# Fused attention and token/channel mixing: the last half of batch 0's attention is added up on VectorE, with another order of loads and conversions around chunk 0

## The chip, the cores and the metric

The kernel runs on one core of a Trainium2 chip. The metric is the device time of one execution in microseconds. The kernel before has a median of 2022.69 us over 3 runs (2022.31 to 2022.91).

## What is computed

The reference, cut to what matters (B=8 batches, S=4096 tokens, D=192 features, H=8 heads, K=7 taps, all fp32):

```python
w = softmax(weight_gen)                      # over the 7 taps, per token and head
x_att[b, s, h, :] = sum_k w[b, s, h, k] * x_pad[b, s + k, h, :]
h = relu(x_att.T @ w_tok1) @ w_tok2          # token mixing: 4096 -> 256 -> 4096
u = x_att + h.T
out = u + relu(u @ w_ch1) @ w_ch2            # channel mixing: 192 -> 1536 -> 192
```

## The kernel before, in words

**Tiles and stages.** A batch is cut into 8 chunks of 512 tokens (`NCH = 8`), so there are 64 chunks, numbered m over all batches. For a chunk, `token1(m)` adds the chunk's share of `x_att.T @ w_tok1` to the sum `th`/`h1s` of its batch; when the eighth chunk of a batch has been added, `make_h1` applies the relu and splits the result into a high and a low fp32r part (`h`). Only then can `token2` of that batch begin: it seeds a PSUM tile `up` with the attention output (`seed_up`), adds `h1 @ w_tok2` to it, and the sum is `u`. The channel mixing of a chunk, in the units (g, p), is products `ph` from `u` and `w_ch1`, a relu and split into `h` by ScalarE (L774) and VectorE (L778), and products `acc` from `h` and `w_ch2`. TensorE matmuls of 64 rows run in pairs on two halves of the array (`emit`, L633).

**Conversions.** The weights arrive raw and are converted in the kernel. A weight block costs three passes on ScalarE (L192, L194, L195) and a shift on VectorE (L191); weights that are split also take a cast to the high part (GpSimd L215 or ScalarE L210) and a subtraction on VectorE (L211; L595 and L596 for `w2s`). `act(what, n)` and `dve(what)` issue the next n passes of a block on that engine, `rest(what)` the rest of its job. The blocks are `("tok", m)` (w_tok1), `("w1", n)` and `("c2", n)` (w_ch1 and w_ch2), `("w2", n)` (w_tok2).

**The prologue, batch 0.** Before any channel mixing, the attention of batch 0 is done in 16 half chunks, i = 0 to 15, in an order written out by hand (tables `loads`, `fetches`, `ahead`, `behind`, `after`, L1144 to L1155). For half i: `product(i)` on VectorE multiplies taps 0 to 4 (L424, 1920 elements a partition), `product_aside(i)` on GpSimd multiplies taps 5 and 6 and adds them (L424, L435), both into the buffer `prk`, of which there are two. `sums(i)` adds the taps on TensorE by transposing matmuls into PSUM (L441, `tapsum`), ScalarE copies the sum (L463), TensorE turns it back (`turn_back`, L441) and ScalarE copies it to `xa` (`keep_turned`, L478). `token1_half(i)` (L1122) multiplies `xa` with the token weights into `th`. The sum is also stored for the residual (`store_sum`, a GpSimd DMA). For the last half, i = 15, VectorE first folds taps 3 to 5 onto 0 to 2 (`fold`, L446), so that TensorE needs 9 matmuls instead of 18. After `token1_half(15)` and four spare matmuls (L1223) comes `make_h1(0)` (ScalarE L609, VectorE L611), `first_token2` (TensorE `acc<-w,h`, L710), `first_u` (ScalarE L726 to L734, VectorE L727 to L733), and then the first `ph` products of chunk 0.

**The steady part.** From there a planner sets the order: it keeps an estimated time for each engine (`at[...]`), and `pump` (L952) places side work (conversions, attention of later batches, output moves L860) from chains by cost and due time. A token1 of a later batch is taken up when its inputs are ready by the planner's estimate (`token1_ready`), in two blocks of 64-row pairs wrapped around channel-mixing units (`emit`, L633). `begin_token2(m)` (L1312) makes sure that the batch's h1 exists: as long as it does not, it issues the missing token1 in one piece, with 128-row matmuls (`whole_token1`, L1305, matmuls on L1303), directly ahead of token2. `TURN` (L672) says behind how many thirds of the `acc` products the first `up` of a chunk is put in chunk 0.

```python
def begin_token2(m):
    need(lambda: m in w2t and m in xbt, ("w2", m))
    while m // NCH not in h1t:
        need(token1_ready, ("w1", state["token1"] + 1), ("x", state["token1"] + 1))
        whole_token1(begin_token1())

def end_token1(tok):
    ...
    pump(end + SLACK_M, (), end + SLACK_A)
    next(tok["it"], None)
```

Of the kernel before, what the change touches and what calls it, by code (L numbers as in the profile page):

```python
# [12 lines left out]
F32 = mybir.dt.float32  # L13
# [10 lines left out]
def mixer_kernel(ctx: ExitStack, tc: tile.TileContext, x, wg, wt1, wt2, wc1, wc2, out):  # L24
    nc = tc.nc
# [390 lines left out]
    def tap_product(i, wn, k0, k1, multiply):  # L416
# [7 lines left out]
        multiply(prt[i][:, k0:k1].rearrange("p k t (h g) -> p k (t h) g", h=H), x_k, w.broadcast_to([P, k1 - k0, HT * H, G]))  # L424
# [18 lines left out]
    def fold(i):  # L443

        pr = prt[i]
        nc.vector.tensor_add(pr[:, 0:FOLD], pr[:, 0:FOLD], pr[:, FOLD:2 * FOLD])  # L446

    def sums(i):
# [4 lines left out]
        for k in range(KD + 1 if i < 2 * NCH - 1 else FOLD):  # L453
            for j in range(NB):
                transpose(ps[:, j * P:(j + 1) * P], flat[:, k, j * P:(j + 1) * P], k + j == 0)
# [17 lines left out]
    def keep_turned(i):  # L473

        m, h = divmod(i, 2)
        if h == 0:
            new_xa(m)
# [194 lines left out]
    TURN = 2  # L672
# [47 lines left out]
    def first_u(up, between):  # L720
# [11 lines left out]
        dve.tensor_copy(hi[e, 1], uc[c])  # L732
        dve.tensor_sub(lo[c, 1], uc[c], hi[c, 1].bitcast(F32))  # L733
# [336 lines left out]
    with tc.tile_pool(name="pro", bufs=1) as pro, \  # L1070
# [42 lines left out]
        def rest(what):  # L1113
            for item in job(what):
                item[2]()

        def token1_half(i):
            m, h = divmod(i, 2)
            w = vals[m][0].rearrange("p (c r) -> p c r", c=CT)
            for r in range(KR):  # L1120
                for c in range(HT * h, HT * h + HT):
                    nc.tensor.matmul(th[:, r, 0:D], w[:, c, r * P:(r + 1) * P], xat[m][:, c, :],  # L1122
                                     start=m + c == 0, stop=m == NCH - 1 and c == CT - 1, skip_group_check=True)
# [5 lines left out]
        def fetch(what):  # L1129
# [48 lines left out]
        for i in range(2 * NCH):  # L1178
# [344 lines left out]
```

## Time and profile before

| | value |
|---|---|
| median of 3 runs | 2022.69 us |
| profiled execution, its own time | 2022.73 us |
| span of that execution | 2021.0 us |
| TensorE busy | 2005.3 us, 99% of the span |
| VectorE busy | 1480.0 us, 73% |
| ScalarE busy | 1297.9 us, 64% |
| GpSimd busy | 240.7 us, 12% |
| granted clock of TensorE, mean | 0.999 |

The profile is of one execution. A row of the timeline is one instruction, or several alike in a row (x8), with its start, its duration, its engine, its line in the code, the tiles out<-in and, in brackets, how long the engine had been idle before it and who released it. Times in the rows count from the span's start; 1.7 us of the execution lie outside the span. A busy time of TensorE says that a matmul was in the pipeline, and an idle time in brackets is where it truly waited.

### The profile page before, as it was taken

The numbers are of one execution on the slowest core, as the hardware profiler recorded it, in microseconds if no ns is written. First come the engines' busy times: TensorE is split into PE (matmuls) and PEld (weight loads), VectorE is DVE, ScalarE is ACT, GpSimd is POOL, SyncE is SP. The second block draws the span as 40 slices with busy tenths as digits, with TensorE's granted clock in tenths as the row PEclk, the third lists the DMA queues.
The fourth block names the chain that finished last, engine by engine and source line by source line (L and its number), as shares of the span: only waits on it lengthen the run. The fifth ranks groups of instructions, "written<-read, shape, count | busy, mean of one in ns | idle before, by whom it ended". The sixth has DMA issues, their size and how long they took to land.

```text
span 2021.0 us, 42824 instructions
## 1 busy us (share of the span) xinstructions
PE 2005.3 (99%) x18123; PEld 1702.3 (84%) x18123; DVE 1480.0 (73%) x1742; ACT 1297.9 (64%) x2033; POOL 240.7 (12%) x304
## 2 busy tenths in 40 slices
PE   9999999999999999999999999999999999999999
PEld 8788899888888888888888888888888888888887
DVE  8789999998877887777887777877777774443433
ACT  7877657566566566566566566566566566566555
POOL 7511111111101110001101011101011100000000
PEclk9999999999999999999999999999999999999999
DMA  9968787887676666676766676766676763222121
GB/s 365 341 200 235 207 232 227 232 222 214 200 211 185 187 186 171 166 212 178 193 186 166 172 206 189 189 184 162 178 211 171 192 162 106 70 74 64 48 66 25
DMA packets 172798, 362.99 MB, mean 180 GB/s; under 512 B 28735, under 2 KB 113983, under 8 KB 156862
## 3 DMA queue, kind: packets, MB, share of 16 engines
q1 hardware_dynamic: 138014, 228.01, 36.7%
q0 software_dynamic: 34304, 132.00, 26.8%
q8 instruction: 143, 2.34, 0.5%
q14 instruction: 49, 0.40, 0.1%
q10 hardware_dynamic: 288, 0.23, 0.0%
HBM read 223.60 MB, written 71.30 MB: 146 GB/s over the span
## 4 chain that ended last, share of the span: by engine, by line
PE 91%; DVE 4%; DMA 2%; ACT 2%; issue 1%; POOL 0%; ACTq 0%; DVEq 0%
PE acc L633 40%; PE ph L633 36%; PE up L633 7%; PE th L633 6%; DMA space<-in_x_dram 1%; DVE prk L424 1%; DVE h L778 1%; DMA s<-vals 1%; DVE pr L282 1%; DMA raw<-in_moe_w_ch_dram 0%; PE tapsum L441 0%; PE acc L1303 0%; DVE val L191 0%; DMA w<-s 0%; PE th L1122 0%
## 5 line engine op out<-in xcount | busy, mean ns | idle before, releaser
L633 PE MATMUL acc<-h,w2s 64*128 64x512 f32 x7500 | 1631.4, 387 | 0.0
L633 PEld LDWEIGHTS acc<-h,w2s 64*128 64x128 f32 x7500 | 1308.6, 184 | 138.8
L633 PE MATMUL ph<-u,w_hi 64*128 64x512 f32 x4608 | 1354.4, 388 | 2.4 <-DVE h L778 1.9
L633 PEld LDWEIGHTS ph<-u,w_hi 64*128 64x128 f32 x4608 | 766.2, 184 | 87.5 <-DVE h L778 3.0
L633 PE MATMUL ph<-u,w_lo 64*128 64x512 f32 x2304 | 803.1, 386 | 0.3 <-DVE w_lo L211 0.3
L774 ACT ACTIVATE h<-ph 128x1024 fp32r<-128x1024 f32 x384 | 393.8, 1026 | 569.0 <-PE ph L633 561.7
L778 DVE SCALAR_TENSOR_TENSOR h<-ph,h 128x1024 fp32r<-128x1024 f32 x384 | 464.7, 1211 | 258.3 <-ACT h L774 257.2
L633 PEld LDWEIGHTS ph<-u,w_lo 64*128 64x128 f32 x2304 | 384.5, 184 | 39.2 <-DVE w_lo L211 0.7
L282 DVE TENSOR_TENSOR pr<-space,wg 128x768 f32<-128x768 f32 x336 | 313.2, 945 | 0.6 <-DMA xa<-pr 0.4
L304 POOL DMA_DIRECT2D xa<-pr x166 | 141.4, 852 | 1357.0 <-DVE pr L296 841.7
L633 PE MATMUL up<-w,h 64*128 64x512 f32 x1240 | 291.5, 386 | 0.0
L633 PEld LDWEIGHTS up<-w,h 64*128 64x128 f32 x1240 | 228.1, 184 | 23.3 <-ACT up L699 0.3
L860 ACT COPY out_tile<-oa 32x256 f32<-32x256 f32 x504 | 203.5, 404 | 6.7
L689 DVE TENSOR_TENSOR uf<-up,uf 64x512 f32<-64x512 f32 x63 | 43.0, 683 | 172.9 <-ACT uf L688 166.9
L296 DVE TENSOR_TENSOR pr<-pr 128x768 f32<-128x768 f32 x168 | 159.2, 948 | 1.9
L633 PEld LDWEIGHTS th<-xh,w 64*128 64x128 f32 x1548 | 119.4, 185 | 7.8
L633 PE MATMUL th<-xh,w 64*128 64x384 f32 (+2 forms) x1548 | 123.5, 298 | 0.0
L860 ACT COPY out_tile<-oc 32x256 f32<-32x256 f32 x252 | 101.5, 403 | 5.7 <-DVE oc L853 1.1
L850 DVE STREAM_TRANSPOSE oa<-acc 128x512 f32<-128x512 f32 x63 | 45.0, 714 | 66.2 <-PE ph L633 63.6
L699 ACT COPY up<-xb 128x1024 f32<-128x1024 f32 x56 | 56.9, 1016 | 34.7 <-DVE h L778 34.7
L841 ACT COPY acc<-uf 128x512 f32<-128x512 f32 x126 | 70.2, 591 | 0.7 <-DVE oa L850 0.3
L282 DVE TENSOR_TENSOR xa<-space,wg 128x768 f32<-128x768 f32 x56 | 53.0, 946 | 4.0 <-DMA space<-in_x_dram 3.8
(126 smaller groups left out, 1338.2 us busy)
## 6 DMA issues: line engine op xcount, KB each, us to landing
w<-s SPq DMA_DIRECT2D x96, 1024.0 KB, 6.4
xa<-pr POOLq DMA_DIRECT2D x166, 384.0 KB, 5.7
space<-in_x_dram POOLq DMA_DIRECT2D x54, 960.0 KB, 8.3
out_dram<-out_tile SPq DMA_DIRECT2D x128, 192.0 KB, 3.3
xb<-xs SPq DMA_DIRECT2D x368, 64.0 KB, 6.4
xs<-t SPq DMA_DIRECT2D x56, 384.0 KB, 3.7
raw<-in_moe_w_tok_dram SPq DMA_DIRECT2D x16, 1024.0 KB, 10.8
s<-w POOLq DMA_DIRECT2D x8, 1024.0 KB, 8.3
```

The costliest lines, as they stand in the source:

```text
L282: nc.vector.tensor_mul(t.rearrange("p t (h g) -> p (t h) g", h=H).rearrange("p (o n) g -> p o n g", o=1), x_k, w)
L296: nc.vector.tensor_add(sums[m], sums[m], prt.pop(m))
L304: nc.gpsimd.dma_start(xat[m].rearrange("p t d -> p (t d)"), sums[m].rearrange("p t d -> p (t d)"), accum_op=ALU.add)
L424: multiply(prt[i][:, k0:k1].rearrange("p k t (h g) -> p k (t h) g", h=H), x_k, w.broadcast_to([P, k1 - k0, HT * H, G]))
L633: ins = nc.tensor.matmul(out_, w, x_, start=start, stop=False, skip_group_check=True).ins
L689: nc.vector.tensor_add(u[c, 1, :], up[c, 1, :], u[c, 1, :])
L699: nc.scalar.copy(up.rearrange("p k (n b c) -> p (k n) c b", c=CT, b=Q), xb.rearrange("p k (n c b) -> p (k n) c b", c=CT, b=Q))
L774: nc.scalar.activation(h[:, :, 0, :], ph, AF.Relu)
L778: nc.vector.scalar_tensor_tensor(h[:, :, 1, :], ph, 0.0, h[:, :, 0, :].bitcast(F32), op0=ALU.max, op1=ALU.subtract)
L841: nc.scalar.copy(acc_t[g][n], u[:, n])
L850: nc.vector.transpose(ua, acc[0])
L860: nc.scalar.copy(dst, src[to:to + Q].rearrange("p (n e d) -> p n e d", n=2, d=Q)[:, n])
```

## The change

**Last half chunk.** `product(15)` no longer goes into `prk` but into the tail of another buffer, `space`. GpSimd multiplies tap 5 into that tail and tap 6 straight into `xa` (`last_aside`), without an add. VectorE adds everything up (`last_sum`): one add of 1152 elements and three of 384. The half reaches `xa` without TensorE and ScalarE. `token1_half(15)` is issued before `token1_half(14)`; three transposes of the finished half (`last_turn`) and a ScalarE copy remain for the store. The four spare matmuls go.

**Loads and conversions.** The third pass of token block 7 moves behind the copy of half 11, its shift from i=15 to i=14; the fetch of `("w2", 1)` moves from i=10 to behind `w1[2]`, `c20` and `c21`; the stores s5 and s6 move to i=14, s7 behind the relu; the loads xb1, x of batch 1 and wg8 move from i=13 and 14 to behind `first_token2`; the conversion of `w1[2]` begins ahead of `first_u`; those of `c2` and `("w2", 1)` are spread over later units. `TURN` goes from 2 to 3.

The diff, cut:

```diff
+    def last_aside(i):
+
+        m, h = divmod(i, 2)
+        new_xa(m)
+        n = 2 * FOLD * HC
+        pr = prt[i] = space[:, 2 * X1 - n:2 * X1].rearrange("p (k t d) -> p k t d", k=2 * FOLD, t=HT)
+        to = xat[m][:, HT * h:HT * h + HT, :]
+        tap_product(i, wnt, KD, KD + 1, nc.gpsimd.tensor_mul)
+        tap_product(i, wnt, KD + 1, K, nc.gpsimd.tensor_mul, to)
+
+    def last_sum(i):
+
+        m, h = divmod(i, 2)
+        pr, to = prt.pop(i), xat[m][:, HT * h:HT * h + HT, :]
+        add = nc.vector.tensor_add
+        add(pr[:, 0:FOLD], pr[:, 0:FOLD], pr[:, FOLD:2 * FOLD])
+        add(pr[:, 0], pr[:, 0], pr[:, 1])
+        add(to, to, pr[:, 2])
+        add(to, to, pr[:, 0])
...
-    TURN = 2
+    TURN = 3
...
-                 9: [w2, "xb0"], 10: [("w2", 1)], 11: [w1[2]], 12: ["c20", ("c2", 1)], 13: ["xb1", 8], 14: ["wg8"]}
-        fetches = {3: ["s0"], 5: ["s1"], 7: ["s2"], 8: ["s3"], 11: ["s4"], 13: ["s5"], 14: ["s6"], 15: ["s7"]}
+                 9: [w2, "xb0"], 11: [w1[2]], 12: ["c20", ("c2", 1)], 13: [("w2", 1)]}
+        fetches = {3: ["s0"], 5: ["s1"], 7: ["s2"], 8: ["s3"], 11: ["s4"], 14: ["s5", "s6"]}
...
-                 11: [(tok[7], 1)], 12: [(w1[1], 1)], 13: [(w2, 1)], 14: [(w2, 1)]}
+                 11: [(tok[7], 1)], 12: [(tok[7], 1), (w1[1], 1)], 13: [(w2, 1)], 14: [(w2, 1)]}
...
-        for i in range(2 * NCH):
+        for i in range(2 * NCH - 1):
...
-        store_sum(i // 2)
-        keep_turned(i)
+        i += 1
+        product(i)
+        last_sum(i)
+        dve(w2)
+        keep_turned(i - 1)
+        seed_up(0, up, xbt[0], (1,))
+        act(w2)
+        token1_half(i)
+        token1_half(i - 1)
+        last_turn(i)
+        dve(w1[0])
+        dve(w2)
+        make_h1(0, th[:, :, 0:D])
+        rest(w1[0])
+        load("s7")
         rest(w2)
-        token1_half(i)
-        spare = ps_pro.tile([P, 512], F32, tag="turn", name="turn", bufs=2)
-        for _ in range(4):
-            nc.tensor.matmul(spare[:, 0:2 * P], w1_hi[:, 0, 0:P], w1_hi[:, 0, 0:2 * P], start=True, stop=True)
-        make_h1(0, th[:, :, 0:D])
+        dve(w1[1])
+        keep_sum(i)
+        act(w1[2], 2)
...
-    first_u(up, lambda: act(w1[2]))
-    act(w1[2], 2)
-    act(c2)
-    rest(w1[1])
-    dve(w1[2])
+    load_xt(1)
+    load_x(NCH)
+    load_wg(NCH)
+
+    def between():
+        act(w1[2])
+        act(c2)
+        rest(w1[1])
+    first_u(up, between, lambda: dve(w1[2]))
+    rest(w1[2])
...
-    state["vals"], state["few"] = 2, 3
+    state["vals"], state["few"] = 1, 2
...
-    first = {0: ((w1[2], ""),), 1: ((c2, "aa"), (c2, "vw")),
-             2: ((c2, ""), (w21, "aaa"), (w21, "vw"), (c21, "aaa"), (c21, "vw"), (w21, ""), (c21, ""), (c22, "aa")),
-             3: ((c22, "a"), (c22, "vw")), 4: ((c22, ""),)}
+    first = {2: ((c2, "aa"), (c2, "vw"), (c21, "aaa"), (c2, ""), (c21, "vw"), (w21, "aa"), (c21, "")),
+             3: ((w21, "a"), (w21, "vw"), (c22, "aa")), 4: ((w21, ""), (c22, "a"), (c22, "vw")), 5: ((c22, ""),)}
```

The new lines shift the old ones: L424 becomes L425, L441 L442, L609 L633, L633 L657, L664 L688, L699 L723, L774 L799, L778 L803, L860 L885 and L1303 L1339.

**What moves.** VectorE at the end of the prologue, from the last token shift (`vals`) to the two splits of h (`h`, L611). Before:

```order
L191 SCALAR_TENSOR_TENSOR vals<-vals,few 128x1024
L424 TENSOR_TENSOR prk<-xt,acc 128x1920 x2
L446 TENSOR_TENSOR prk<-prk 128x1152
L191 SCALAR_TENSOR_TENSOR vals<-vals,few 128x1024
L191 SCALAR_TENSOR_TENSOR val<-val,few 128x1024
L191 SCALAR_TENSOR_TENSOR val<-val,few 128x768 x2
L211 TENSOR_TENSOR w_lo<-val,w_hi 128x3x256
L211 TENSOR_TENSOR w_911<-val,w_911 128x1024
L611 SCALAR_TENSOR_TENSOR h_927<-th,h_927 128x2x128
```

And now:

```order
L425 TENSOR_TENSOR prk<-xt,acc 128x1920
L191 SCALAR_TENSOR_TENSOR vals<-vals,few 128x1024
L425 TENSOR_TENSOR space<-xt,acc 128x1920
L459 TENSOR_TENSOR space<-space 128x1152
L460 TENSOR_TENSOR space<-space 128x384
L461 TENSOR_TENSOR xa<-xa,space 128x384
L462 TENSOR_TENSOR xa<-xa,space 128x384
L191 SCALAR_TENSOR_TENSOR val<-val,few 128x1024
L191 SCALAR_TENSOR_TENSOR val<-val,few 128x768
L211 TENSOR_TENSOR w_880<-val,w_880 128x1024
L635 SCALAR_TENSOR_TENSOR h_896<-th,h_896 128x2x128
```

The last product has left `prk`, the fold is followed by three adds, and one shift and one split have moved behind the splits of h.

ScalarE around the first relu and u, from the copy of half 14 (`xa`) on. Before:

```order
L478 COPY xa<-turn 128x384
L463 COPY sum<-tapsum 128x3x128
L697 COPY acc<-xb_77 128x8x64
L210 CAST w_911<-val 128x1024
L478 COPY xa<-turn 128x384
L609 ACTIVATE h_927<-th 128x2x192
L726 CAST u<-acc 128x512
L728 COPY uf<-acc 64x512
L192 ACTIVATE few<-raw 128x768
L731 CAST u<-uf 64x512
L734 CAST u<-u 64x512
L194 ACTIVATE few<-raw 128x768
```

And now:

```order
L502 COPY xa<-turn 128x384
L721 COPY acc<-xb_77 128x8x64
L210 CAST w_880<-val 128x1024
L633 ACTIVATE h_896<-th 128x2x192
L487 COPY sum<-tapsum 128x3x128
L192 ACTIVATE few<-raw 128x768
L194 ACTIVATE few<-raw 128x768
L750 CAST u<-acc 128x512
L752 COPY uf<-acc 64x512
L195 ACTIVATE val<-raw 128x768
L192 ACTIVATE few<-space 128x768
L755 CAST u<-uf 64x512
```

The copy of the last sum has moved behind the relu, the copy of the last turn is gone, and four conversion passes stand ahead of the second u cast where one stood.

The end of batch 1, just ahead of token2 of chunk 8. ScalarE before, from the copy of the last token sum (`h1s`) on:

```order
L664 COPY h1s<-th 128x2x192
L609 ACTIVATE h_3937<-h1s 128x2x192
L699 COPY up<-xb_77 128x8x4x32
L774 ACTIVATE h<-ph 128x2x512
L860 COPY out_tile<-oc 32x8x32 x2
L860 COPY out_tile<-oa 32x8x32 x4
L860 COPY out_tile<-oc 32x8x32 x2
```

And now, from the copy of the last but one token sum:

```order
L688 COPY h1s<-th 128x2x192
L668 COPY th<-h1s 128x2x192
L885 COPY out_tile<-oc 32x8x32 x2
L885 COPY out_tile<-oa 32x8x32 x4
L885 COPY out_tile<-oc 32x8x32 x2
L885 COPY out_tile<-oa 32x8x32 x4
L688 COPY h1s<-th 128x2x192
L633 ACTIVATE h_3964<-h1s 128x2x192
L723 COPY up<-xb_77 128x8x4x32
L799 ACTIVATE h<-ph 128x2x512
```

TensorE in the same place, now:

```order
L657 MATMUL acc<-h,w2s 128x512
L657 MATMUL ph<-u,w_hi 128x512
L1339 MATMUL th<-xa,val 128x192 x8
L657 MATMUL up<-w_3595,h_3964 128x512
L657 MATMUL acc<-h,w2s 128x512
L657 MATMUL up<-w_3595,h_3964 128x512
```

The last token1 of the batch (m=15) has become one whole block directly ahead of the `up` matmuls that need its relu, and twelve output moves stand ahead of the copy that starts that relu. The end of batch 2 (m=23, 16 matmuls) has the same form; in the kernel before, neither batch has it.

## Rows read from the trace of the kernel before

**Rows 1.** The page: busy time of each engine, share of the span, instructions.

```profile
PE 2005.3 (99%) x18123; PEld 1702.3 (84%) x18123; DVE 1480.0 (73%) x1742; ACT 1297.9 (64%) x2033; POOL 240.7 (12%) x304
```

**Rows 2.** Waits of TensorE, 75 us to the end: total us, times, longest.

```profile
PE ph L633 <- DVE h L778: 1.9, 3, 1.2
PE th L633 <- ACT th L644: 1.4, 1, 1.4
```

**Rows 3.** Windows: length, busy PE, PEld, DVE, ACT, POOL, clock, DMA share, GB/s.

```profile
110.00:220.00 110.00, 109.77 (x996) 91.66 (x998) 103.25 (x123) 84.36 (x127) 15.95 (x22) 1.00 0.78 214
```

**Rows 4.** Timeline of VectorE, end of the prologue: start us, us, instruction.

```profile
59.60 2.14 DVE L424 TENSOR_TENSOR prk<-xt,acc 128x1920 f32<-128x1920 f32 x1
64.11 2.15 DVE L424 TENSOR_TENSOR prk<-xt,acc 128x1920 f32<-128x1920 f32 x1 [2.37 <-POOL prk L435]
67.40 1.36 DVE L446 TENSOR_TENSOR prk<-prk 128x1152 f32<-128x1152 f32 x1 [1.14 <-POOL prk L435]
68.68 1.22 DVE L191 SCALAR_TENSOR_TENSOR vals<-vals,few 128x1024 uint32<-128x1024 uint32 x1
```

**Rows 5.** Line L668 (a VectorE add of 384): duration ns min/median/max.

```profile
L668 DVE TENSOR_TENSOR h1s<-h1s x6: 545/546/548, 555.4 to 1771.8; 128x384 f32<-128x384 f32 x6
```

**Rows 6.** Timeline of TensorE from the last token products to chunk 1.

```profile
70.06 1.52 PE L1122 MATMUL th<-xa,vals 128*128 128x192 f32 x8
71.42 0.49 PE L441 MATMUL turn<-ident,sum 128*128 128x128 f32 x3
72.64 1.57 PE L1122 MATMUL th<-xa,vals 128*128 128x192 f32 x8 [0.72 <-ACT xa L478]
74.78 2.96 PE L710 MATMUL acc<-w,h 128*128 128x512 f32 x10
77.67 0.50 PE L633 MATMUL ph<-u,w_hi 64*128 64x512 f32 x2
...
86.14 0.50 PE L633 MATMUL ph<-u,w_hi 64*128 64x512 f32 x2 [1.25 <-DVE h L778]
```

**Rows 7.** Timeline of ScalarE around the first relu and u.

```profile
72.10 0.48 ACT L478 COPY xa<-turn 128x384 f32<-128x384 f32 x1
74.24 0.49 ACT L609 ACTIVATE h<-th 128x384 fp32r<-128x384 f32 x1 [1.66 <-PE th L1122]
77.00 0.59 ACT L726 CAST u<-acc 128x512 fp32r<-128x512 f32 x1 [2.27 <-PE acc L710]
78.31 0.90 ACT L192 ACTIVATE few<-raw 128x768 uint32<-128x768 uint32 x1
...
81.18 1.07 ACT L194 ACTIVATE few<-raw 128x768 f16<-128x768 f32 x1
```

**Rows 8.** Timeline of GpSimd, products of the last half.

```profile
64.58 1.70 POOL L424 TENSOR_TENSOR prk<-xt,wg 128x384 f32<-128x384 f32 x2
66.36 1.01 POOL L435 TENSOR_TENSOR prk<-prk 128x384 f32<-128x384 f32 x1
```

**Rows 9.** Timeline of TensorE at the ends of batches 1 and 2.

```profile
305.26 1.46 PE L633 MATMUL th<-xa,val 64*128 64x192 f32 x15
306.43 0.52 PE L633 MATMUL ph<-u,w_hi 64*128 64x512 f32 x1
...
583.95 0.41 PE L633 MATMUL ph<-u,w_hi 64*128 64x512 f32 x1
...
588.29 0.39 PE L633 MATMUL up<-w,h 64*128 64x512 f32 x1
```

**Rows 10.** Timeline of ScalarE at the ends of batches 1 and 2.

```profile
308.84 0.48 ACT L664 COPY h1s<-th 128x384 f32<-128x384 f32 x1 [0.33 <-PE th L633]
...
310.27 1.02 ACT L699 COPY up<-xb 128x1024 f32<-128x1024 f32 x1 [0.40 <-DVE h L778]
...
584.15 0.80 ACT L664 COPY h1s<-th 128x768 f32<-128x768 f32 x1
```

**Rows 11.** Line L860 (output moves): duration ns min/median/max.

```profile
L860 ACT COPY out_tile<-oa x504: 401/403/409, 122.3 to 2006.6; 32x256 f32<-32x256 f32 x168
```

More of the change, by code (lines that the diff above doesn't have):

```diff
@@ L414, in mixer_kernel, with tap_product @@
     FOLD = (KD + 1) // 2
-    def tap_product(i, wn, k0, k1, multiply):
+    def tap_product(i, wn, k0, k1, multiply, to=None):
         m, h = divmod(i, 2)
@@ L423, in tap_product @@
         w = w[:, j * CT + HT * h:j * CT + HT * h + HT, :, first:first + k1 - k0].rearrange("p t (h o) k -> p k (t h) o", o=1)
-        multiply(prt[i][:, k0:k1].rearrange("p k t (h g) -> p k (t h) g", h=H), x_k, w.broadcast_to([P, k1 - k0, HT * H, G]))
+        to = prt[i][:, k0:k1] if to is None else to.rearrange("p (o t) d -> p o t d", o=1)
+        multiply(to.rearrange("p k t (h g) -> p k (t h) g", h=H), x_k, w.broadcast_to([P, k1 - k0, HT * H, G]))
     def product(i):
@@ L441, in transpose, with last_turn @@
         nc.tensor.matmul(out, data, ident, is_transpose=True, start=start, stop=True, skip_group_check=True)
-    def fold(i):
-        pr = prt[i]
-        nc.vector.tensor_add(pr[:, 0:FOLD], pr[:, 0:FOLD], pr[:, FOLD:2 * FOLD])
+    def last_aside(i):
[14 more added lines that the diff above has]
+        add(to, to, pr[:, 0])
+    def last_turn(i):
+        m, h = divmod(i, 2)
+        ps = sum_ps[i] = ps_pro.tile([P, 512], F32, tag="sum", name="tapsum", bufs=2)
+        flat = xat[m][:, HT * h:HT * h + HT, :].rearrange("p t d -> p (t d)")
+        for j in range(NB):
+            transpose(ps[:, j * P:(j + 1) * P], flat[:, j * P:(j + 1) * P], j == 0)
     def sums(i):
@@ L452, in sums @@
         flat = pr.rearrange("p k t d -> p k (t d)")
-        for k in range(KD + 1 if i < 2 * NCH - 1 else FOLD):
+        for k in range(KD + 1):
             for j in range(NB):
@@ L475, in keep_turned @@
         m, h = divmod(i, 2)
-        if h == 0:
+        if m not in xat:
             new_xa(m)
@@ L718, in new_u, with first_u @@
         return t[:, 0], t[:, 1]
-    def first_u(up, between):
+    def first_u(up, between, then):
         hi, lo = new_u(0)
@@ L732, in first_u @@
         dve.tensor_copy(hi[e, 1], uc[c])
+        then()
         dve.tensor_sub(lo[c, 1], uc[c], hi[c, 1].bitcast(F32))
@@ L1122, in token1_half @@
                     nc.tensor.matmul(th[:, r, 0:D], w[:, c, r * P:(r + 1) * P], xat[m][:, c, :],
-                                     start=m + c == 0, stop=m == NCH - 1 and c == CT - 1, skip_group_check=True)
+                                     start=m + c == 0, stop=i == 2 * NCH - 2 and c == HT - 1, skip_group_check=True)
         def store_val(m):
@@ L1188, in mixer_kernel @@
                 run(islice(soft[i // 4 + 1], 3))
-            if i == 2 * NCH - 1:
-                fold(i)
             for what in after.get(i, ()):
                 dve(what)
-            if i == 15:
-                rest(w1[0])
             sums(i)
-            if i + 1 < 2 * NCH:
-                product_aside(i + 1)
+            (product_aside if i < 2 * NCH - 2 else last_aside)(i + 1)
             if i > 0:
@@ L1234, in mixer_kernel @@
     land_c2(2, "out", out_tile)
-    first_u(up, lambda: act(w1[2]))
-    act(w1[2], 2)
-    act(c2)
-    rest(w1[1])
-    dve(w1[2])
+    load_xt(1)
[7 more added lines that the diff above has]
+    rest(w1[2])
     nc.gpsimd.memset(uf_[0][DC:P, 1, :], 0.0)
+    store_sum(NCH - 1)
     load_xt(2)
-    state["vals"], state["few"] = 2, 3
+    state["vals"], state["few"] = 1, 2
     state["jobs"] = deque((convert_w2, i) for i in range(2, NCH))
```

4 lines of the change are left out of this document (2 added, 2 removed).

## The prediction, made blind

> **What bounds the kernel now.** I read the page first: TensorE is busy 99% of the span, VectorE 73%, ScalarE 64% [rows 1]. So the time changes only where TensorE's work or its waits change. Next the waits of TensorE behind the prologue: only a few microseconds in all, 1.9 for VectorE's h in three places and one wait of 1.4 for a ScalarE copy of `th` [rows 2]. The change can gain little there; what it can gain is the pace of the prologue's end, and what it can lose is new waits. A window shows the one stretch where another engine is as full as TensorE: from 110 to 220 us VectorE works 103.25 of 110.00 us [rows 3]. The timelines then give the chain at the end of the prologue: VectorE waits 2.37 us for a `prk` buffer that GpSimd holds, and 1.14 us more before the fold [rows 4]; TensorE adds and turns, ScalarE copies `xa` until 72.58, the last token product runs, and the relu starts at 74.24 [rows 6, 7]. All sums are against the profiled execution, 2022.73 us, which is 0.04 above the median.
>
> **1. The last half on VectorE: -2.7.** The product of half 14 ends at 61.74 (59.60 + 2.14). The next product does not need `prk` now, so the wait of 2.37 goes; the shift of 1.22 that stood behind the fold comes first, to 62.96, then the product of 2.15, to 65.1 [rows 4]. GpSimd's first product (tap 5, half of 1.70) is there at about 65.4 and its second at 66.3; the add of 1.01 is gone [rows 8]. So the fold of 1.36 runs from 65.4 to 66.8 [rows 4]. The three adds of 384 elements have no row of their own; the nearest row is another VectorE add of 128x384 with 0.55 each [rows 5], so `xa` is ready at about 68.4, where the ScalarE copy had it at 72.58 [rows 7]. Who is late next is half 14: its `xa` comes by TensorE and ScalarE as before, and its product started at 70.06 [rows 6]. That is why the order of the two matters: product 15 now runs in front of it (1.36 us from start to the turn behind, 70.06 to 71.42 [rows 6]), product 14 behind, done at about 71.5. The relu then starts at about 71.55 in place of 74.24. The following `acc` started 0.54 after the relu and the first `ph` 2.89 after that [rows 6]; kept, the first `ph` is at 75.0 in place of 77.67. Ahead of the u cast ScalarE now does the copy of the last sum (about 0.48) and two passes of 0.90 and 1.07. From 71.55 they and the relu (0.49) last until 74.5; the cast started 2.76 after the relu, which would be 74.3 [rows 7]. So 0.2 at most of that is in the way.
>
> Behind that, TensorE waits 1.25 before 86.14 for VectorE's first h [rows 6]. The second u block comes later relative to `ph` (four conversion passes on ScalarE ahead of its cast where one was), the splits of weights come earlier; I expect one pause of about that size in chunk 0 again, a little earlier or later. So I take the gain of the first `ph` as it is, **-2.7**. Bounds: -4.0 if that pause of 1.25 goes as well, and -0.5 if the later `up` seed and the later u block give back nearly all.
>
> **2. Edits at nothing.** The four spare matmuls ran while TensorE waited for the relu. The fetch of `("w2", 1)` now stands on SP's queue behind the last pass of `w1[2]`; its first reader is a conversion in a later unit, and if that cover fails its price is some tenths, inside the bounds of part 1. On GpSimd's queue the stores s5 to s7 pass the last products: the second product has over a microsecond in hand before the adds need it. The loads of xb1, of batch 1's x and of wg8 leave SP's queue earlier and come back behind `first_token2`; their readers are the second `up` and batch 1's attention. `TURN` puts ten `up` matmuls behind forty `acc` instead of thirty; the number of matmuls is the same, and the seed gets more time.
>
> **3. The wait of 1.4 for `th`: -0.6.** That copy stood on ScalarE behind casts of u [rows 2]. In the new order fewer casts stand ahead of it. Bounds: 1.4 gained, or 0.5 lost where another block meets the same queue. I take a little under half, because token blocks of batch 1 still meet casts of u.
>
> **4. The end of batch 1: +2.7.** The planner now takes up the last token1 of batch 1 too late to wrap it, and issues it whole, directly ahead of the `up` that needs its relu. TensorE runs its queue in order, so it has nothing to do from the end of `th` until this chain is done: start of the copy 0.33 after `th`, copy 0.48, relu 0.49 (the same line in the prologue), seed 1.02 [rows 7, 10]. That is 2.3. Before, a whole unit lay in that gap. The twelve output moves ahead of the copy last 12 x 0.403 = 4.84 [rows 11]; they start behind two copies at about 309.8 and are done at 314.7, while the unit of over 4.3 and the whole block end later, so they cost nothing here. The block itself: two prologue products of the same size from start to start, 2 x 1.36 = 2.7 [rows 6], against two wrapped blocks of 1.17 each (305.26 to 306.43 [rows 9]), 0.36 more. Together **+2.7**; bounds +2.0 (half the seed runs ahead of the relu's end) and +3.2 (the moves are late).
>
> **5. The end of batch 2: +3.8.** The same form with wider tiles: copy 0.80 [rows 10], an add of 0.55 on VectorE [rows 5], relu about 0.5, seed 1.02, and 0.33 ahead: 3.2. Here the moves are late: from 584.15 the copy, a cast and a copy of the same width (about 0.8 each) and 4.84 of moves end at 591.4; the unit from 583.95 to 588.29 and a block of 2.7 end at 591.0 [rows 9, 10]. That makes 3.4, and the block itself 0.36 more. **+3.8**; bounds +3.0 and +4.4.
>
> **The sum.** -2.7 - 0.6 + 2.7 + 3.8 = +3.2, that is 2022.73 + 3.2 = **2025.9 us**. Within 0.2%, about 4 us (2018.7 to 2026.7), this kernel's measurement can hardly tell it from no change. The forecast's own range, from half of each bound, is 2023.5 to 2028.0.
>
> **Rivals.**
>
> *The early gain is kept in full (chance 0.18).* The pause of 1.25 in chunk 0 and the wait of 1.4 both go, and the batch ends cost 2.7 and 3.6: 2022.73 - 4.0 - 1.4 + 6.3 = 2023.6. For it: the weights' splits and the h of chunk 0 have more slack behind an earlier relu [rows 4, 6]. Against: the pause hangs on VectorE's h, whose queue holds what was moved behind `first_u`.
>
> *VectorE gives the early gain back (0.18, slower).* The conversions of c2 and `("w2", 1)` move from the first units into later ones, up to 220 us, where VectorE has only 110.00 - 103.25 = 6.75 us free [rows 3]. If the moved shifts and splits (1.22 each [rows 4]) come in front of h, TensorE waits for h there. It decides from the point where five or six of them fall into that stretch. Then -2.7 and -0.6 are gone: 2022.73 + 6.5 = 2029.2. Against: TensorE waited only 1.9 us for h in the whole run [rows 2].
>
> *The sum is not earlier (0.07, slower).* If GpSimd's products for half 15 land as late as its add did (67.4 [rows 4, 8]), or VectorE's adds cost twice the row's 0.55, `xa` is no earlier than half 14's, and the relu gains nothing: 2022.73 - 0.6 + 6.5 = 2028.6.
>
> *The clock falls behind the new pauses (0.05, slower).* The longest waits in the rows are 1.25 to 1.4 us and the granted clock is 1.00 around them [rows 2, 3, 6]; a pause of 3.4 has no row. If the clock went to 1.2 GHz after the pause of batch 2, a unit of 4.3 us [rows 9] would take as long again: 2025.9 + 4.3 = 2030.2. The Trainium skill ("TensorE: Matmul & The Clock Gate", Part 1: The HAM clock gate) says that the clock is halved after TensorE has been idle for a while. It speaks against this change, but no row here shows a halved clock behind a wait, so it gets a small chance.
>
> *The batch ends cost only half (0.06, faster).* If each pause were half as long and the early gain whole: 2022.73 - 5.4 + 3.1 = 2020.4 or less.
>
> **How the numbers follow.** The forecast has 0.46, of which about 0.06 lies above 2026.7. Slower: 0.18 + 0.07 + 0.05 + 0.06 = 0.36. Faster by over 0.2% needs over 4 us, more than all of the early bounds less one batch end: 0.06. The rest, 0.58, is within 0.2%. The range goes from 2020.4 (the last rival) to 2029.6 (VectorE's rival with a little above it); the clock's case and the faster tail are left out.
>
> **What would show it.** Right: the first `ph` near 75.0; whole `th` matmuls of batch 1 and 2 with a wait of TensorE for the `up` seed or h of 2.3 and 3.4 us behind each; no other new wait over 1 us; granted clock 1.00. Wrong: no wait at those two places, waits for h between 110 and 220 us, or a first `ph` at 77.

## The result, and the profile after

The changed kernel takes 2033.08 us (median of 6 runs, 2032.06 to 2034.6), the kernel before 2022.72 us (6 runs, 2022.31 to 2022.91). The ratio is 1.0052, 95% interval 1.0039 to 1.0065: about 10.4 us slower, outside the range of the prediction. The profiled execution took 2034.60 us with a span of 2032.8 us.

The page and the waits of TensorE behind 70 us, which answer to [rows 1, 2]:

```profile
PE 2010.5 (99%) x18078; PEld 1689.3 (83%) x18078; DVE 1485.0 (73%) x1745; ACT 1298.3 (64%) x2032; POOL 239.4 (12%) x303
```

```profile
PE up L657 <- ACT up L723: 6.3, 2, 4.0
PE ph L657 <- DVE h L803: 3.2, 3, 2.2
```

The wait of 1.4 for the copy of `th` is gone. In its place stand two waits for the seed of `up`, 6.3 us together, and one of 2.2 for h. TensorE is also busy 5.2 us longer (2010.5 against 2005.3) on 45 recorded matmuls fewer. Where the time came in is read from the first `up` matmul of each chunk in the two timelines of TensorE (the end is that of the twentieth):

| chunk | `up` before, us | `up` after, us | later by |
|---|---|---|---|
| 2 | 120.96 | 119.14 | -1.8 |
| 3 | 149.06 | 148.33 | -0.7 |
| 6 | 246.16 | 243.74 | -2.4 |
| 7 | 279.51 | 279.62 | +0.1 |
| 8, start | 312.88 | 315.61 | +2.7 |
| 8, end | 317.60 | 322.06 | +4.5 |
| 9 | 343.39 | 345.46 | +2.1 |
| 15 | 527.36 | 529.56 | +2.2 |
| 16, start | 557.77 | 566.63 | +8.9 |
| 16, end | 562.47 | 574.32 | +11.9 |
| 62 | 1943.45 | 1955.32 | +11.9 |

Behind chunk 16 nothing changes any more. From chunk 9 to 15 the change looks 2.4 us better than it is, since the wrapped token blocks of batch 2 run one chunk later there and one of them is still owed. So the ledger of this execution is: up to chunk 7, +0.1; the start of chunk 8, +2.6; its twenty `up` matmuls, which take 6.45 in place of 4.72, +1.7; then to the start of chunk 16 from +4.5 to +8.9, +4.4; its `up`, 7.69 in place of 4.70, +3.0. Together 11.8.

The two places in the timeline of TensorE, and ScalarE's chain in each:

```profile
310.45 2.87 PE L1339 MATMUL th<-xa,val 128*128 128x192 f32 x16
315.61 0.50 PE L657 MATMUL up<-w,h 64*128 64x512 f32 x1 [2.30 <-ACT up L723]
...
560.07 2.52 PE L1339 MATMUL th<-xh,w 128*128 128x384 f32 x16
566.63 0.79 PE L657 MATMUL up<-w,h 64*128 64x512 f32 x1 [4.04 <-ACT up L723]
```

```profile
311.94 1.65 ACT L885 COPY out_tile<-oa 32x256 f32<-32x256 f32 x4
313.62 0.48 ACT L688 COPY h1s<-th 128x384 f32<-128x384 f32 x1
314.12 0.52 ACT L633 ACTIVATE h<-h1s 128x384 fp32r<-128x384 f32 x1
314.56 1.01 ACT L723 COPY up<-xb 128x1024 f32<-128x1024 f32 x1
...
562.04 1.65 ACT L885 COPY out_tile<-oa 32x256 f32<-32x256 f32 x4
563.72 0.80 ACT L688 COPY h1s<-th 128x768 f32<-128x768 f32 x1
565.14 0.52 ACT L633 ACTIVATE h<-h1s 128x384 fp32r<-128x384 f32 x1 [0.62 <-DVE h1s L692]
565.57 1.01 ACT L723 COPY up<-xb 128x1024 f32<-128x1024 f32 x1
```

At the second place TensorE ends the whole block at 562.6, ScalarE's copy starts only at 563.72 because the output moves last until then, and the add, the relu and the seed follow. A window table shows what the pauses left behind (columns as in [rows 3]; the clock is the number ahead of the last two):

```profile
314.00:316.00 2.00, 0.39 (x4) 0.34 (x6) 0.63 (x2) 1.97 (x4) 0.00 (x0) 1.00 1.01 199
316.00:318.00 2.00, 2.00 (x16) 1.58 (x14) 1.46 (x2) 1.44 (x2) 0.00 (x0) 0.69 0.98 320
318.00:320.00 2.00, 2.00 (x14) 1.55 (x12) 2.00 (x3) 0.00 (x0) 0.00 (x0) 0.50 0.93 228
320.00:322.00 2.00, 2.00 (x20) 1.69 (x18) 0.63 (x1) 0.00 (x0) 0.00 (x0) 0.96 0.98 408
...
566.00:570.00 4.00, 3.37 (x16) 2.68 (x18) 2.77 (x5) 2.24 (x3) 0.00 (x0) 0.50 1.03 262
570.00:574.00 4.00, 4.00 (x26) 3.10 (x26) 1.38 (x2) 0.00 (x0) 0.85 (x1) 0.65 1.02 377
```

A granted clock of 0.50 is 1.2 GHz in place of 2.4. From 316 to 322 and from 570 to 574 TensorE is busy all the time, and its busy share alone would not tell that it gets less done: 14 matmuls in the 2 us from 318, at a clock of 0.50, and 20 in the 2 us from 320, at 0.96.

The early gain is there at first. From chunk 2 to chunk 3 it shrinks from 1.8 to 0.7; TensorE waits for u at 133.22 and 134.36 there, 0.5 us together, and the trace has no wait for the rest. Without the wait for `th` it is 2.4 at chunk 6. In chunk 6 it goes, where VectorE stands in front of a load of x with an h queued behind it (VectorE, then TensorE):

```profile
266.48 0.96 DVE L282 TENSOR_TENSOR xa<-space,wg 128x768 f32<-128x768 f32 x1 [3.47 <-DMA space<-in_x_dram]
...
269.22 1.22 DVE L803 SCALAR_TENSOR_TENSOR h<-ph,h 128x1024 fp32r<-128x1024 f32 x1
```

```profile
270.49 0.50 PE L657 MATMUL ph<-u,w_hi 64*128 64x512 f32 x2 [2.21 <-DVE h L803]
```

The size of this wait is one execution's: it is 1.68 at the same place in the trace of the run filled below, whose order is the same up to there.

### The profile page after: what moved, and what is told of

Same layout as the page of the kernel before. It is cut to its first block, busy times and chain, and to the rows that moved or that the text cites. A ratio compares the mean times of both kernels' runs of the same rounds, so it can differ in the third digit from the quotient of the medians.

```text
span 2032.8 us, 42739 instructions
## 1 busy us (share of the span) xinstructions
PE 2010.5 (99%) x18078; PEld 1689.3 (83%) x18078; DVE 1485.0 (73%) x1745; ACT 1298.3 (64%) x2032; POOL 239.4 (12%) x303
## 4 chain that ended last, share of the span: by engine, by line
PE 91%; DVE 5%; ACT 2%; DMA 1%; issue 0%; POOL 0%; SPq 0%; ACTq 0%; DVEq 0%
PE acc L657 40%; PE ph L657 36%; PE up L657 7%; PE th L657 6%; ACT out_tile L885 1%; PE tapsum L442 1%; DVE h L803 1%; PE th L1147 1%; PE acc L1339 1%; DVE pr L282 1%; DMA space<-in_x_dram 1%; DVE prk L425 1%; DVE pr L296 0%; DMA xb<-xs 0%; ACT h L799 0%
## 5 line engine op out<-in xcount | busy, mean ns | idle before, releaser
L657 PE MATMUL acc<-h,w2s 64*128 64x512 f32 x7500 | 1635.8, 387 | 0.0
L657 PEld LDWEIGHTS acc<-h,w2s 64*128 64x128 f32 x7500 | 1309.6, 185 | 144.3 <-DVE h L803 0.2
L657 PE MATMUL ph<-u,w_hi 64*128 64x512 f32 x4608 | 1354.3, 388 | 4.5 <-DVE h L803 3.2
L657 PEld LDWEIGHTS ph<-u,w_hi 64*128 64x128 f32 x4608 | 765.5, 184 | 96.4 <-DVE h L803 5.1
L657 PE MATMUL ph<-u,w_lo 64*128 64x512 f32 x2304 | 802.9, 386 | 0.0
L799 ACT ACTIVATE h<-ph 128x1024 fp32r<-128x1024 f32 x384 | 393.8, 1026 | 577.7 <-PE acc L657 416.9
L803 DVE SCALAR_TENSOR_TENSOR h<-ph,h 128x1024 fp32r<-128x1024 f32 x384 | 464.8, 1211 | 263.5 <-ACT h L799 262.3
L657 PEld LDWEIGHTS ph<-u,w_lo 64*128 64x128 f32 x2304 | 384.6, 184 | 42.1
L657 PE MATMUL up<-w,h 64*128 64x512 f32 x1240 | 295.7, 391 | 6.3 <-ACT up L723 6.3
L657 PEld LDWEIGHTS up<-w,h 64*128 64x128 f32 x1240 | 231.2, 187 | 32.2 <-ACT up L723 7.1
L885 ACT COPY out_tile<-oa 32x256 f32<-32x256 f32 x504 | 203.6, 404 | 6.7
L657 PEld LDWEIGHTS th<-xh,w 64*128 64x128 f32 x1516 | 116.7, 185 | 7.9
L657 PE MATMUL th<-xh,w 64*128 64x384 f32 (+1 forms) x1516 | 120.8, 298 | 0.0
L885 ACT COPY out_tile<-oc 32x256 f32<-32x256 f32 x252 | 101.6, 403 | 5.6 <-DVE oc L878 1.1
L723 ACT COPY up<-xb 128x1024 f32<-128x1024 f32 x56 | 56.9, 1017 | 32.9 <-DVE h L803 32.8
```

The costliest lines, as they stand in the source:

```text
L657: ins = nc.tensor.matmul(out_, w, x_, start=start, stop=False, skip_group_check=True).ins
L723: nc.scalar.copy(up.rearrange("p k (n b c) -> p (k n) c b", c=CT, b=Q), xb.rearrange("p k (n c b) -> p (k n) c b", c=CT, b=Q))
L799: nc.scalar.activation(h[:, :, 0, :], ph, AF.Relu)
L803: nc.vector.scalar_tensor_tensor(h[:, :, 1, :], ph, 0.0, h[:, :, 0, :].bitcast(F32), op0=ALU.max, op1=ALU.subtract)
L885: nc.scalar.copy(dst, src[to:to + Q].rearrange("p (n e d) -> p n e d", n=2, d=Q)[:, n])
```

## The experiments

**Theory A**: the loss is the two whole token blocks at the ends of batches 1 and 2, with their pauses and the halved clock behind them. **Theory B**: VectorE is late with batch 1's attention because conversions were moved behind chunk 0; the whole blocks are only the sign, and other waits take their place where they are wrapped again. All medians, each with the kernel before as it ran beside it:

| kernel | us | before, us | ratio (95%) |
|---|---|---|---|
| the change | 2033.08 | 2022.72 | 1.0052 (1.0039 to 1.0065) |
| wrap_both | 2027.53 | 2023.11 | 1.0021 (1.0012 to 1.0030) |
| wrap_first | 2028.36 | 2023.11 | 1.0028 (1.0017 to 1.0039) |
| filled | 2028.90 | 2023.11 | 1.0029 (1.0017 to 1.0041) |
| before_whole | 2032.29 | 2023.11 | 1.0043 (1.0028 to 1.0057) |
| turn2 | 2026.80 | 2023.20 | 1.0015 (1.0006 to 1.0024) |
| old_first | 2023.82 | 2023.20 | 1.0005 (0.9996 to 1.0014) |
| old_first_turn2 | 2021.75 | 2023.20 | 0.9993 (0.9984 to 1.0001) |
| last_half_alone | 2023.59 | 2023.20 | 1.0001 (0.9992 to 1.0010) |
| turn2_x12 | 2024.94 | 2024.19 | 1.0010 (1.0001 to 1.0019) |
| old_first_turn2_x12 | 2022.59 | 2024.19 | 0.9994 (0.9985 to 1.0003) |
| th_copy_first | 2020.56 | 2023.43 | 0.9985 (0.9976 to 0.9994) |
| old_first_turn2_again | 2021.04 | 2023.43 | 0.9989 (0.9980 to 0.9997) |

### The whole blocks in the kernel before

```diff
-                if token1_ready(100 if following else 6 * STEP) and ready[0][0] <= g + NCH + (not following or g % NCH == NCH - 2):
+                if token1_ready(100 if following else 6 * STEP) and ready[0][0] not in (2 * NCH - 1, 3 * NCH - 1) and ready[0][0] <= g + NCH + (not following or g % NCH == NCH - 2):
```

> The kernel before, in which the planner is kept from wrapping m=15 and m=23: the two blocks come out whole in front of token2 of their batches, as in the change, and nothing of the prologue is changed. Theory A: the same price as in the change, 8 to 12 us: 2031 to 2035 us. Theory B: the kernel before has its attention in time, so the pauses are only the chain of copies, without the clock: 2027 to 2029 us.

2032.29 us, 9.2 above the kernel before. The prologue is untouched here, so the two blocks alone cost nearly as much as the whole change. Its timeline of TensorE and windows behind the first pause (one) and the second (two):

```profile
317.82 0.50 PE L633 MATMUL up<-w,h 64*128 64x512 f32 x1 [2.09 <-ACT up L699]
...
568.07 0.79 PE L633 MATMUL up<-w,h 64*128 64x512 f32 x1 [3.00 <-ACT up L699]
```

```profile
319.00:321.00 2.00, 2.00 (x12) 1.55 (x10) 2.00 (x2) 0.63 (x1) 0.00 (x0) 0.50 0.93 303
...
569.00:571.00 2.00, 2.00 (x12) 1.51 (x10) 2.00 (x2) 1.60 (x2) 0.00 (x0) 0.50 1.08 246
...
573.00:575.00 2.00, 2.00 (x21) 1.80 (x19) 0.08 (x1) 0.42 (x1) 0.14 (x1) 1.00 0.95 238
```

Theory A has the price right. B's number (2027 to 2029, with no halved clock where attention is in time) is wrong: the clock fell behind both pauses here too.

### The pauses filled

```diff
         end_token1(tok)
+        for _ in range(18 if tok["m"] < F1 * NCH else 34):
+            nc.tensor.matmul(acc_t[tok["m"] - NCH][0][:, 0:P], w1_hi[:, 0, 0:P], nought, start=False, stop=False,
+                             skip_group_check=True)
```

> The change, with 18 and 34 matmuls of 128 columns that add zeros to acc, put into TensorE's queue right behind the two whole blocks, where it waits anyway. They move nothing else. If the clock falls because TensorE rests there, the clock stays at 1.00 and the 1.7 and 3.0 us of half speed go: 2028 to 2029 us, with the pauses' time itself unchanged. If the clock falls for another reason (the switch to whole 128-row blocks, the transfers in flight), the time stays at 2032 to 2034 us.

`nought` is a tile of zeros that ScalarE writes once. 2028.90 us: 5.8 above before where the change is 10.4 above. The rows of TensorE and the windows behind the pauses:

```profile
561.70 3.93 PE L1350 MATMUL acc<-nought,w_hi 128*128 128x128 f32 x34
565.90 0.50 PE L658 MATMUL up<-w,h 64*128 64x512 f32 x1 [0.28 <-ACT up L724]
```

```profile
316.00:318.00 2.00, 2.00 (x21) 1.63 (x20) 1.81 (x2) 1.10 (x2) 0.00 (x0) 1.00 0.96 300
...
567.00:570.00 3.00, 3.00 (x30) 2.83 (x28) 3.00 (x4) 0.52 (x1) 0.00 (x0) 1.00 1.00 365
```

The seed comes no earlier, but the clock stays at 1.00, and the `up` matmuls of chunks 8 and 16 take 4.82 and 4.85 us in place of 6.45 and 7.69. So the halved clock hangs on TensorE's rest, and its price was 1.6 + 2.8 us; the medians, each against its own runs of the kernel before, say about the same: 10.4 - 5.8 = 4.6.

### One block wrapped, both wrapped

The planner's own estimate says why the blocks are whole. When it asks for a token block, the block's attention output must be ready no later than 0.1 us behind TensorE's estimated time where another unit follows. At the two questions for m=14 the change has (times in ns by the planner's account):

```
ready 210933, asked at 209832, allowed 100:  not taken
ready 210933, asked at 222771:               taken, half a chunk late
```

Before, the first question was at 207418 with the block ready at 199385. A miss of 1.0 us in an estimate thus makes m=15 whole; batch 2 then starts one chunk late and m=23 is whole too. In wrap_first the first limit is 1500 in place of 100 (the first line added), in wrap_both the other limit is 20 steps in place of 6 (the second):

```diff
-                if token1_ready(100 if following else 6 * STEP) and ready[0][0] <= g + NCH + (not following or g % NCH == NCH - 2):
+                if token1_ready(1500 if following else 6 * STEP) and ready[0][0] <= g + NCH + (not following or g % NCH == NCH - 2):
+                if token1_ready(100 if following else 20 * STEP) and ready[0][0] <= g + NCH + (not following or g % NCH == NCH - 2):
```

> The change, with another number of the planner altered (1500 ns in place of 100 where a unit follows): only the block at the end of batch 1 is wrapped again, the one at the end of batch 2 stays whole. Theory A: the pause of 2.3, the 0.3 of the block and the 1.7 of halved clock go, about 4.3 less than the change: 2028.5 to 2029.5 us. If the two ends depend on each other, or the clock behind the second end costs otherwise, it lies elsewhere. Theory B: no gain, 2032 to 2034 us.

2028.36 us, 5.3 above before: wrapping the end of batch 1 gives back 5.1 of the 10.4, where theory A said about 4.3 (its range began at 2028.5), and the end of batch 2 keeps its pause (3.95 us in this trace, with a clock of 0.53 behind it).

> The change, with one number of the planner altered: the last token1 of a chunk is taken up a little before its inputs are ready by the estimate (20 steps in place of 6), so that m=15 and m=23 are wrapped around units again, as before. Theory A (the loss is the two whole blocks at the ends of batches 1 and 2: pauses of 2.3 and 4.0 us, the halved clock behind them, 1.7 and 3.0, and the blocks themselves): the 11 us go, 2021 to 2023.5 us, granted clock 1.00 throughout. Theory B (VectorE's attention of batch 1 is late, the whole blocks are only its sign): TensorE waits for xa or th of the wrapped blocks in place of them, 2027 us or more.

2027.53 us, with runs from 2024.37 to 2032.45. No block is whole, the clock is 1.00, yet only 6.0 of the 10.4 us are gone. Theory A's number is missed, and B has a part in it: blocks are taken up early, m=9 above all, and TensorE waits elsewhere, longest for the seed of the `up` of chunk 4, behind an h on VectorE:

```profile
184.55 0.50 PE L657 MATMUL up<-w,h 64*128 64x512 f32 x1 [1.54 <-ACT up L721]
```

Most of the loss comes later than this wait, and later than batch 1's attention: at chunk 8 this timeline is 0.6 behind the kernel before (313.49 against 312.88), at chunk 16 4.0 (561.74 against 557.77). From chunk 9 to 13 it has waits of TensorE for h of at most 0.67, which make up only part of that; the rest stays open.

### The conversions and TURN

Three ways back that leave the last half on VectorE: `TURN` at 2 (turn2), the old table of conversions (old_first), and both.

```diff
-    TURN = 3
+    TURN = 2
...
-    first = {2: ((c2, "aa"), (c2, "vw"), (c21, "aaa"), (c2, ""), (c21, "vw"), (w21, "aa"), (c21, "")),
-             3: ((w21, "a"), (w21, "vw"), (c22, "aa")), 4: ((w21, ""), (c22, "a"), (c22, "vw")), 5: ((c22, ""),)}
+    first = {1: ((c2, "aa"), (c2, "vw")),
+             2: ((c2, ""), (w21, "aaa"), (w21, "vw"), (c21, "aaa"), (c21, "vw"), (w21, ""), (c21, ""), (c22, "aa")),
+             3: ((c22, "a"), (c22, "vw")), 4: ((c22, ""),)}
```

> The change with TURN back at 2 and nothing else. In the planner's own estimate the change misses the moment to take up m=14 by 1.0 us (ready at 210.93, asked at 209.83 with 0.1 allowed), and everything after it is half a chunk late; with TURN at 2 the estimate is met and no block is whole. Theory A: the 11 us of the two ends go, 2020.5 to 2023.5 us. Theory B (the conversions that were moved behind chunk 0 make VectorE late whatever the planner believes): TensorE waits for h, up or th of batch 1 instead, 2025 us or more.

2026.80 us, within B's number: no whole block, but TensorE waits elsewhere. VectorE again stands in front of a load of x (the first row), and TensorE misses the `up` of chunk 12 behind it (the second). The longest wait is another, for the seed of chunk 1's `up` (the third), which stands on ScalarE behind conversion passes:

```profile
435.50 0.96 DVE L282 TENSOR_TENSOR xa<-space,wg 128x768 f32<-128x768 f32 x1 [2.94 <-DMA space<-in_x_dram]
```

```profile
438.69 0.49 PE L657 MATMUL up<-w,h 64*128 64x512 f32 x1 [2.04 <-ACT up L723]
...
100.72 2.51 PE L1339 MATMUL up<-w,h 128*128 128x512 f32 x10 [2.19 <-ACT up L721]
```

With `TURN` at 3, in the change, that third wait is 0.80. It costs less than its length: from the first `ph` to the `up` of chunk 2 turn2 takes 44.0 us, old_first_turn2 43.3. The larger part comes late, as in wrap_both: at chunk 8 the timeline is 0.6 ahead of the kernel before, at chunk 16 4.9 behind (562.63 against 557.77).

> The change with TURN at 3, but the conversions of c2 and w2 around chunk 0 spread over its units as before (from unit 1 to 4 in place of 2 to 5). The planner wraps both blocks again. Theory A: 2020.5 to 2023.5 us, as with TURN at 2. Theory B: this is the one that helps, 2021 to 2023 us, while TURN alone does not. If the fetch of w2's block 1, which now comes late, holds the earlier conversions up, TensorE waits for h in chunk 0 or for up of chunk 1, and it is 2024 us or more.

2023.82 us, the same as before within the interval, and 0.8 above B's range: the conversions decide more than `TURN`, as B says. What keeps it from a gain is `TURN` at 3, which puts the second `up` ten matmuls later, so that u of chunk 1 is late for its `ph`:

```profile
110.44 0.50 PE L657 MATMUL ph<-u,w_hi 64*128 64x512 f32 x1 [1.49 <-DVE u L776]
...
117.60 0.49 PE L657 MATMUL ph<-u,w_hi 64*128 64x512 f32 x1 [1.19 <-DVE h L803]
```

> The change with both put back: from chunk 1 on the planner's order is then that of the kernel before, unit by unit, and what is left of the change is the prologue: the last half on VectorE, the order of loads, the conversions ahead of u. Whatever differs from before is the prologue's own worth. From the trace of the change (first ph 1.8 us earlier, up of chunk 2 1.8 earlier): 2020.5 to 2022 us. If the order of loads gives it back, 2022.5 to 2024 us.

2021.75 us, and 2021.04 in a second run, 1.4 and 2.4 under the kernel before beside them. The first interval, 0.9984 to 1.0001, just holds 1; the second, 0.9980 to 0.9997, lies below it, with a gain a little above what was expected of it. The planner's order is then that of before, and this is what the prologue's change is worth.

> The kernel with the old spread of conversions and TURN at 2 once more, on the chip of the run beside it, as what that one is compared with: 1.0 to 2.0 us under the kernel before.

### The load of x counted longer

`LOAD_X` from 9000 to 12000 (ns), on top of turn2 and of old_first_turn2.

> The change with TURN at 2, and the planner counts 12 us in place of 9 for a load of x, so that VectorE's attention that needs it is not put ahead of an h before it can have landed. In the run with TURN at 2 VectorE waited 2.9 us at 435 for a load of x with an h queued behind it, and TensorE 2.0 us for the up behind that. Theory (what is left of that kernel's loss is VectorE standing in front of a load of x that takes longer than planned): waits of VectorE for x of under 1 us, 2024 to 2025.5 us, and less spread. If the loss lies in the conversions themselves (VectorE too full), TensorE waits elsewhere and it stays at 2026 to 2028 us.

2024.94 us, 0.8 above the kernel before beside it, where turn2 was 3.6 above. The wait of VectorE at that place is 1.82 in place of 2.94, that of TensorE 0.93 in place of 2.04. The direction is as expected, but a wait for x of over 1 us remains, the wait for the seed of chunk 1's `up` is as long as in turn2 (2.17), and the runs still spread from 2023.7 to 2029.47.

> The kernel with the old spread of conversions and TURN at 2 (1.4 us faster than before so far), also with 12 us for a load of x. Its VectorE waited only 0.8 us for x, with no wait of TensorE behind it, so there is little to win: 2021 to 2022.5 us if the planner's number only matters where attention is late. If the longer count makes the attention of batch 1 late in general, 2023 us or more.

2022.59 us, 1.6 under the kernel before beside it: no more than without the longer count.

### The last half alone

The kernel before with `last_aside`, `last_sum`, the order of the two token products and no spare matmuls as in the change, x of chunk 8 loaded later, everything else as before.

> The kernel before, with the last half on VectorE, its token product first, no spare matmuls, and the one load that this forces (x of chunk 8, which lands where the products now lie) behind the first token2; all other loads, conversions and TURN as before. The sum itself should bring the relu 1.5 to 2.5 us earlier. If the other order of loads is not needed for the gain: 2020 to 2021.5 us. If the gain of the last half is taken back by what was left in front of u (the shift and the splits on VectorE, as before): 2022 to 2023.5 us.

2023.59 us, no difference. The timelines of TensorE and VectorE show why:

```profile
70.65 4.52 PE L1146 MATMUL th<-xa,vals 128*128 128x192 f32 x16 [1.92 <-DVE vals L191]
```

```profile
65.70 2.01 DVE L459 TENSOR_TENSOR space<-space 128x1152 f32<-128x1152 f32 x1 [1.69 <-POOL space L425]
...
69.28 1.22 DVE L191 SCALAR_TENSOR_TENSOR vals<-vals,few 128x1024 uint32<-128x1024 uint32 x1
```

The sum is ready at 69.3, but the token weights' shift, left where it was, now stands behind it, and TensorE waits for that. Moving the shift ahead of the sum is part of the gain.

### A version faster than both

The wait of 1.4 in [rows 2] is still in old_first_turn2 (1.25 at 222.9). There ScalarE casts u three times ahead of the copy of `th`; in th_copy_first the copy of m=11 goes first:

```diff
+                early = following and ready and ready[0][0] == 11
+                if early and token1_ready(100) and ready[0][0] <= g + NCH + (g % NCH == NCH - 2):
+                    tok = begin_token1()
                 pump(done_at + (TOP + SLACK if following else 300), soon, done_at - 900)
```

> The kernel with the old spread of conversions and TURN at 2, and in one place, the token block m=11, ScalarE copies th ahead of the three casts of u behind which it stood. TensorE waited 1.25 us at 222.9 for that copy (1.40 in the kernel before). If that wait is lost time: it goes, 2020.3 to 2021.2 us on a chip where the kernel before takes 2022.7. If the casts that now come 0.5 us later hold up the next u, TensorE waits for u instead, and nothing is gained: 2021.5 to 2022.5 us.

2020.56 us, ratio 0.9985 (0.9976 to 0.9994), 2.9 under the kernel before beside it. It is 0.5 under old_first_turn2 on the same chip, less than the wait of 1.25, and the runs of the two overlap (2019.94 to 2022.4 and 2020.74 to 2022.99), so that this last step alone is not shown to gain. TensorE's largest waits behind 75 us are then these, and the one for `th` is not among them:

```profile
PE ph L657 <- DVE h L803: 0.7, 3, 0.3
PE ph L657 <- DVE u L776: 0.7, 2, 0.5
PE acc L1340 <- DVE w2s L619: 0.4, 1, 0.4
```

## Why the prediction was wrong

**Part 1, the last half on VectorE: right in mechanism, too large, and then lost.** The first `ph` came at 75.86, not at 75.0: 1.8 us gained in place of 2.7. (This is one pair of executions: the eleven traces with this prologue have the first `ph` at 75.59 to 76.97, the two with the old one at 77.67 and 80.22.) The term that was mis-sized is the shift of 1.22 [rows 4], read where GpSimd computed nothing. Moved ahead of the last product it runs beside GpSimd's product and add, and takes 2.37; the fold takes 1.58 in place of 1.36:

```profile
61.76 2.37 DVE L191 SCALAR_TENSOR_TENSOR vals<-vals,few 128x1024 uint32<-128x1024 uint32 x1
64.05 2.14 DVE L425 TENSOR_TENSOR space<-xt,acc 128x1920 f32<-128x1920 f32 x1
66.30 1.58 DVE L459 TENSOR_TENSOR space<-space 128x1152 f32<-128x1152 f32 x1
67.91 0.56 DVE L460 TENSOR_TENSOR space<-space 128x384 f32<-128x384 f32 x1
...
75.86 0.49 PE L657 MATMUL ph<-u,w_hi 64*128 64x512 f32 x2 [0.19 <-issue]
```

The trace of the kernel before has the same pair a little earlier, with the same effect, and the prediction did not use it:

```profile
57.73 1.95 DVE L191 SCALAR_TENSOR_TENSOR vals<-vals,few 128x1024 uint32<-128x1024 uint32 x1
58.66 1.88 POOL L435 TENSOR_TENSOR prk<-prk 128x384 f32<-128x384 f32 x1
```

So `xa` was ready at 69.5 in place of 68.4 and the relu started at 72.55 in place of 71.55. The adds were right (0.56 against 0.55). The 2.4 us by which chunk 6 came earlier were then lost in chunk 6. I had this as VectorE's rival (0.18): too many conversions in front of h. What the trace shows is a different wait, a load of x, that meets an h in VectorE's queue. That the moved conversions bring such waits about is shown by turn2 and old_first_turn2, which differ in their table alone: 3.6 us above the kernel before with the moved table, 1.4 below it with the old one. By which steps they do it was not traced.

**Part 2.** "Edits at nothing" holds for the matmuls and stores. It was wrong for `TURN` and the conversions. Together they have no price where they stand (from the first `ph` to the `up` of chunk 2 it is 43.28 us, before 43.29), though each alone has one, the waits of old_first and turn2 in chunks 0 and 1. But both move the planner's estimates, and with them the token blocks of two batches.

**Part 3.** The wait of 1.4 went in full, where I took 0.6; like the rest of the early gain, that was lost by chunk 7.

**Part 4, the end of batch 1: right.** The pause is 2.30 (predicted 2.3), the start of chunk 8 moved by 2.6 (predicted 2.7). One step in it was luck: the moves were to be done well before the block, but they end at 313.59 and the block at 313.32, just when the copy could start anyway.

**Part 5, the end of batch 2: the mechanism right, the size a little low, the rows in the wrong place.** The pause is 4.04 (predicted 3.4, though the terms given for it, 0.4 and 2.87, make 3.3), with the block 4.4 (3.8). The rows at 583.95 to 588.29 and 584.15 [rows 9, 10] belong to chunk 17, one chunk behind the end of batch 2, whose token2 starts at 557.77; I took them for that end. At the true place the copy of `th` waits for VectorE, the moves end 1.1 us behind the block in place of 0.4, and the chain behind them takes the 2.9 of the sum.

**The clock: the step that failed most.** I gave it 0.05, because the waits in the rows, up to 1.4 us, had left the clock at 1.00, and I priced it at one end only. It fell behind both pauses, 1.7 and 3.0 us in this execution. The Trainium skill ("TensorE: Matmul & The Clock Gate", Part 1: The HAM clock gate) says that the clock is halved when TensorE has been idle; the trace agrees at both places, though not behind every pause (the last section), and the filled pauses show that it is the rest that does it. With pauses of a length that no row showed, that rule deserved more than a small chance. Of the 8.7 us between my sum (+3.2) and this execution (+11.9), the clock is 4.7, the early gain that did not stay 3.4 (-3.3 forecast, +0.1 at chunk 7), and the size of the second end 0.6. The median of the change is 1.5 below this execution, so these shares are of one execution.

The sum's own range was added up wrong as well: half of each bound gives 2024.1 to 2028.1, not 2023.5 to 2028.0. Nothing else rests on it.

## What to carry to other kernels

Where a planner's estimates set the order, an edit has two prices: that of its instructions, and that of the order that comes out of it; look for work that was interleaved and now stands in one piece in front of what needs it. A pause of TensorE costs its own length and can cost half speed behind it; work that keeps it busy there, even useless work, can be cheaper than rest. A gain in a prologue lasts only if the next engine in line, here VectorE with its queue in fixed order, is not late for something else.

## What was not expected of the hardware

**The length of a pause alone did not tell whether the clock fell.** It fell behind pauses of 2.09 (before_whole), 2.30 and 4.04 us (the change), and stayed at 1.00 behind 2.21 us in the change (at 270.49) and behind 2.19 and 2.04 us in turn2 (at 100.72 and 438.69). What sets these apart was not tried.

**VectorE and GpSimd slow each other in some pairs of operations and not in others.** The shift L191 takes 1.22 us alone and 2.37 beside GpSimd's work; GpSimd's add takes 1.01 alone [rows 8] and 1.89 beside that shift:

```profile
63.11 1.89 POOL L436 TENSOR_TENSOR prk<-prk 128x384 f32<-128x384 f32 x1
64.96 0.86 POOL L425 TENSOR_TENSOR space<-xt,wg 128x384 f32<-128x384 f32 x1
```

The product of 1920 elements that follows on VectorE takes 2.14, as before [rows 4], with GpSimd at work as well. The Trainium skill ("GPSIMD Engine Reference", section 1, Specifications) says that GpSimd shares its interfaces to SBUF with VectorE, with contention for VectorE instructions in a 2-port perf mode or with two inputs in SBUF. The rows agree on both: the shift has two inputs in SBUF (`vals`, `few`), the product only one (`xt`), since its other input (`acc`) lies in PSUM.
